# Windowed attention and a gated FFN on one core: four chunk pairs in place of three, and probabilities scaled in float32

## The chip, the cores and the metric

The kernel runs on one core of a Trainium2 chip. The metric is device time in microseconds (us), from start to end of one execution; lower is better. The engines are TensorE (PE in the profile; its weight loads are PEld), VectorE (DVE), ScalarE (ACT), GpSimd (POOL) and SyncE (SP, which here issues nearly all DMAs).

## What is computed

Attention with a window of 31 keys and block summaries (4 batches, 8 heads, 768 positions, head size 64), and behind it an FFN over the 3072 tokens (512 to 2048 to 512). Cut to what matters:

```python
k_sum = k.reshape(B, H, 24, 32, D).max(axis=3)
v_sum = v.reshape(B, H, 24, 32, D).mean(axis=3)
scores_l = scale * q @ k.T                      # kept where |i - j| < 16
scores_s = scale * q @ k_sum.T + log(32)
a = softmax(concat([scores_l, scores_s]))       # over 768 + 24 keys
x = a @ concat([v, v_sum])                      # 3072 x 512 after a transpose
h = x @ w_in                                    # 3072 x 2048
out = (h / (1 + exp(-h)) * h) @ w_out           # 3072 x 512
```

## The kernel before

**Tiling.** The tokens are 24 stages of 128 (`s`, six to a batch) and 12 chunks of 256 (`c`, two stages each). The hidden width is 8 groups of 256 (`f`). Operands that must keep more than float16 are split into a high and a low float16 part, and a product is three float16 matmuls (high by high, low by high, high by low).

**Attention** of a stage (`job_a`, `normal`, `job_c`): scores into PSUM (L697, 12 matmuls of 182 columns for four heads), a masked minimum on DVE (L708), the exponential with its sum on ACT (L711), then `normal` for two heads at a time: scale by the reciprocal of the sum into float16 (`times`, on DVE, ACT or POOL), the low part on DVE (`rest_of`, L276), a DMA transpose of both parts, and the product with V (L786). `job_v` and `v_scale` make the block means and the scale of V for a batch, `job_k` and `job_scale` those of K and Q.

**FFN.** `job_f` works one chunk and one group: the first product (L982, 24 matmuls of 256 columns), tanh on ACT (L996), a product on DVE (L997), a split on ACT and DVE or POOL, and the second product (L991, 12 of 512 columns). Chunks 0 to `WCH` - 1 go that way. From chunk `WCH` = 6 on, `pair_f` takes two chunks and one group at once: seven block products in place of eight (L1053, 42 matmuls of 256 columns where two `job_f` issue 48), with sums of blocks taken on the way (L1079, L1081, copies by L265), and the same second product (L1101). It needs sums of blocks of w_in, which `sum_w` makes once for each of the eight groups (four additions, L870, a high part on ACT and a low part on DVE), spread over the chunks from 2 to `WCH` - 1, and sums of blocks of x, made by `pair_x` for every pair.

**Order.** All steps are registered with the engines that may run them and a cost. `ORDER` is a table that fixes the engine and the place of every step; `Plan.replay` reads it and each engine's instructions are issued in that order, with warming matmuls (L391, `fill`) put where it leaves PE unused. Each engine works strictly in order, and SP issues its DMAs in order as well.

Of the kernel before, what the change touches and what calls it, by code (L numbers as in the profile page):

```python
# [21 lines left out]
P = 128  # L22
# [33 lines left out]
WCH = 6  # L56
# [198 lines left out]
def local_attn_ffn(ctx: ExitStack, tc: tile.TileContext, q0, qkT, qF, qkD, kF, v, vR, w, out):  # L255
# [118 lines left out]
    e_t = ring(NE, [P, 2, NKEY], F32, "e")  # L374
# [132 lines left out]
    def v_scale(b, prio):  # L507
        k = sbank()
# [6 lines left out]
            lambda e: nc.vector.tensor_scalar(out=sc2[:, 1:2], in0=sc2[:, 1:2], scalar1=XTOP, scalar2=None, op0=ALU.mult),  # L515
# [9 lines left out]
    def job_v(b, prio):  # L525
        prio += nudge("v", b)
        for j in range(4):
            stg, key = staging()
            vr = stg[:, :S]
            plan.op({"dma": 1020}, lambda e, vr=vr, j=j: nc.sync.dma_start(out=vr, in_=vR[b, :, j, :]), w=key, prio=prio)  # L530
            plan.op({"dve": 869}, lambda e, vr=vr, j=j: nc.vector.tensor_reduce(out=vm_t[:, j, :], in_=vr.rearrange("p (n k) -> p n k", k=BLK), axis=AX.X, op=ALU.add),
                    r=key, w=[("vm", j)], prio=prio, port=())
            plan.op({"dve": 869}, lambda e, vr=vr, j=j: nc.vector.tensor_reduce(out=am_t[:, j:j + 1], in_=vr, axis=AX.X, op=ALU.max, apply_absolute_value=True), r=key, w=[("am", j)], prio=prio, port=())
        am_sum(4, prio)
        k = sbank()
# [9 lines left out]
        v_scale(b, prio)  # L545
# [115 lines left out]
    def job_a(m, prio):  # L661
# [37 lines left out]
        if g % 2 == 0:  # L699
# [6 lines left out]
            plan.op({"pe": 600 if b else 950 if plain else 820}, scores, r=need, w=[("bank", x) for x in pair_banks], prio=prio, cols=728)  # L706
# [24 lines left out]
        for x in (m - 1, m):  # L731
            normal(x, su, sums, prio)

    def normal(m, su, sums, prio):
        n, pk = m % NE, m % NP
        et, pt = e_t[n], p_t[pk]
        er = [("e", n, 0), ("e", n, 1)]
        tt, ttk = tt_of(m)
        c0 = m % 2 * 2

        def scaled(e, i):
            by = su[:, c0 + i:c0 + i + 1]
            times(e, pt[:, i, :NKEY], et[:, i, :NKEY], by)
# [4 lines left out]
        def low(e):  # L748
            for i in range(2):
                rest_of(pt[:, i, P + 64:P + 64 + NKEY], et[:, i, :NKEY], su[:, c0 + i:c0 + i + 1], pt[:, i, :NKEY])  # L750

        plan.op({"dve": 680}, low, r=er + sums, w=[("p", pk), ("p", pk, "half")], prio=prio)
        plan.op({"dma": 672}, lambda e: nc.sync.dma_start_transpose(out=tt, in_=pt.rearrange("p a b -> p (a b)")), r=[("p", pk), ("p", pk, "half")], w=[ttk], prio=prio, cols=1230)
# [365 lines left out]
    def job_stage(s):  # L1119
# [20 lines left out]
        job_vs(s, p[0] - TUNE["vs"] if b else p[0])  # L1140
# [68 lines left out]
    "1la1lm1m900400v01100l1lz1lh01f00r00b00h1m601k01501b01p05p07007605w06q06w02y02401t02j07i06606203908j02808t03s06c08p07807p"  # L1209
    "06e0aq03d08z09102n07z08507v0200990av06l02f0re07g09i08709n0b908f0ga0d204303202u0rl0ca0bq09s0ck0dj0rr03o0d90b005g0ed04d0gf"  # L1210
    "0bg0e303h03w09x0bw0cg0dp0df0cq10a0e90ej0ru0dr0tm10n1nh0el04904g0dy10h0bm0es04n04s05l0f204x0520cs11t0b50gt0by10q0080f7057"
    "05c0a00d01nm0h00v50i40gk0tt0s00ha09b0a70tz0fc0hu0fh0hg0u20ia0i00sx0ic0s40u70h60hi0s70lu0c60fk0ik0hq1200ac0ai0im0se1261nu"
    "0fr0jn0jt0gp0it0jx0ev0ue0iz0k30j30lz0k50j91nx0km0vc0sj0kr0sp0kw0jb0l10kc0uf0l40fw0ao0ji0lb0vh0md0ta0kf0g20st0g80t40um0ux"
    "0mu0ne0nk0n01cw1410no0nu0nw12i0mk0vu0mq0n21480o40na12p0m41290v10vl0td1d11d912v0o61uk1dv14q10v0ph0w10w70pn0m91dd1dj0on0od"
    "0p70oj0pd0ot0wa0wg12y1e01dl0q60pp1up0wk0ov0pw0ut0wn0wu1120lg1ux14d0p30y20x10x51dq1330pz0qb1521e80xd0x91eu1ez0lm0qg1ec0y9"
    "1ei0yf14h0xk0ql18h0yi1f70qo0xq0qv0yo1fb1fh1ek0xt14x0tj0ys1n40r00zl1u80ls1vj1ep0yv1fo0z21v01tn0r61fj1mu0ra12f0zd1381561h2"
    "1h70zs0zh15b0vr1hf1131mn18o16916m1hj1ft1hp1fy18u1v41tq16g15i11a13b18x13i1vy1w41hw1j015j0z91g611l1ga0zy1n71ty1gg10116p363"
    "16y1751791md3681j50xz1gn10717e1ml1i11jd16v14n17j1mx15q17o1i61ie1tg1va1931gi1ii1io17r3bf3bk1hr3bn11h1vg13p13t1wd17y19736d"
    "19c1iv1jh1jn11p1831lu1uh19f19m19r19w1a11a61891wa1ab1ag18d1jz1k41o01o71ne13x1b11ju1or1kc1c51wj1x21h01cf1oh1bv1iq1yz1z41b5"
    "1ox1wp1kg1km1vp1jp1p11xc1kt20336k15x1611vv1lr1c91bz1zc1ws44e1x91zg1xs1651zm1p71zs1od1on1xj1l51qn1re1r41qu1pb4s22081wz1rk"  # L1220
# [122 lines left out]
```

## Time and profile before

| | us |
|---|---|
| median of 3 runs (605.93 to 606.89) | 606.72 |
| the profiled execution, whole | 605.51 |
| its span, first to last instruction | 603.8 |
| PE busy | 594.7 |
| PEld busy | 400.1 |
| DVE busy | 462.7 |
| ACT busy | 403.3 |
| POOL busy | 157.0 |

The share of an engine's busy time is taken over the span. Matmuls overlap, so the mean duration of one matmul is longer than the distance from one to the next; the time that a run of them takes is read from where the next piece begins.

### The profile page before, as it was taken

The numbers are of one execution on the slowest core, as the hardware profiler recorded it, in microseconds if no ns is written. First come the engines' busy times: TensorE is split into PE (matmuls) and PEld (weight loads), VectorE is DVE, ScalarE is ACT, GpSimd is POOL, SyncE is SP. The second block draws the span as 40 slices with busy tenths as digits, with TensorE's granted clock in tenths as the row PEclk, the third lists the DMA queues.
The fourth block names the chain that finished last, engine by engine and source line by source line (L and its number), as shares of the span: only waits on it lengthen the run. The fifth ranks groups of instructions, "written<-read, shape, count | busy, mean of one in ns | idle before, by whom it ended". The sixth has DMA issues, their size and how long they took to land.

```text
span 603.8 us, 13503 instructions
## 1 busy us (share of the span) xinstructions
PE 594.7 (98%) x5052; PEld 400.1 (66%) x5052; DVE 462.7 (77%) x1237; ACT 403.3 (67%) x929; POOL 157.0 (26%) x206
## 2 busy tenths in 40 slices
PE   8999999999999999999999899999999999999997
PEld 5786666676676776666676566765666765777653
DVE  7998989999878848987989689989877586464330
ACT  4999999767777577676787568677656475343321
POOL 3336412321422022313321404120333234300100
PEclk9999999999999999999999999999999999999999
DMA  8898724564596651765596355826445424000001
GB/s 324 307 403 334 311 62 145 105 216 105 134 198 125 192 187 53 211 166 96 165 216 129 121 176 127 213 79 138 151 107 160 59 81 80 36 36 1 1 1 70
DMA packets 85558, 87.88 MB, mean 146 GB/s; under 512 B 66780, under 2 KB 68828, under 8 KB 83444
## 3 DMA queue, kind: packets, MB, share of 16 engines
q1 hardware_dynamic: 85348, 86.89, 51.1%
q8 instruction: 39, 0.64, 0.4%
q14 instruction: 27, 0.22, 0.1%
q10 hardware_dynamic: 144, 0.13, 0.1%
HBM read 62.82 MB, written 6.29 MB: 114 GB/s over the span
## 4 chain that ended last, share of the span: by engine, by line
PE 93%; DMA 3%; DVE 1%; ACT 1%; issue 0%; SPq 0%
PE bank L991 22%; PE bank L1101 21%; PE bank L982 19%; PE bank L1053 18%; PE bank L786 4%; PE bank L697 3%; DMA wt<-in_w_dram 1%; PE bank L689 1%; PE bank L770 1%; DMA wt<-in_kF_dram 1%; DMA raw<-in_vR_dram 1%; PE bank L720 1%; PE bank L391 1%; DMA out_dram<-raw 1%; PE bank L611 0%; PE bank L722 0%
## 5 line engine op out<-in xcount | busy, mean ns | idle before, releaser
L991 PE MATMUL bank<-wt,g 128*128 128x512 f16 (+1 forms) x544 | 141.9, 406 | 0.8 <-ACT g L269 0.8
L982 PE MATMUL bank<-xh,wt 128*128 128x256 f16 x768 | 136.2, 273 | 0.0
L982 PEld LDWEIGHTS <-wt 128*128 128x128 f16 x1152 | 111.5, 98 | 25.0 <-issue 3.8
L1053 PE MATMUL bank<-wt 128*128 128x256 f16 x936 | 114.4, 273 | 1.1 <-DVE t L1033 0.8
L1053 PEld LDWEIGHTS <-wt 128*128 128x128 f16 x936 | 90.8, 98 | 24.9 <-issue 1.7
L982 PE MATMUL bank<-xl,wt 128*128 128x256 f16 x384 | 104.7, 273 | 0.0
L711 ACT ACTIVATE e<-e,mx 128x182 f32<-128x182 f32 x192 | 83.6, 437 | 24.3 <-DVE mx L708 22.1
L991 PEld LDWEIGHTS <-g 128*128 128x128 f16 x480 | 45.8, 98 | 47.2 <-issue 0.2
L1032 ACT ACTIVATE t<-bank,asc 128x512 f32<-128x512 f32 x48 | 32.4, 686 | 59.1 <-PE bank L1053 48.7
L279 POOL TENSOR_TENSOR g<-t,g 128x512 f16<-128x512 f32 x34 | 39.4, 1159 | 123.5 <-ACT g L1034 47.7
L1101 PE MATMUL bank<-wt,g 128*128 128x512 f16 x288 | 69.3, 379 | 0.0
L276 DVE SCALAR_TENSOR_TENSOR p<-e,sum,p 128x182 f16<-128x182 f32 x160 | 59.7, 419 | 4.2 <-ACT p L269 2.0
L708 DVE CUSTOM_DVE_ANT_0 e<-bank,masks,qsc 128x182 f32<-128x182 f32 x144 | 52.5, 401 | 3.6 <-PE bank L697 2.9
L996 ACT ACTIVATE t<-bank,asc 128x512 f32<-128x512 f32 x48 | 32.7, 681 | 28.9 <-PE bank L982 26.8
L271 POOL TENSOR_SCALAR p<-e,sum 128x182 f16<-128x182 f32 x52 | 23.1, 449 | 106.6 <-ACT t L1032 13.5
L1033 DVE SCALAR_TENSOR_TENSOR t<-t,bank 128x512 f32<-128x512 f32 x48 | 32.4, 684 | 22.1 <-ACT t L1032 21.8
L1101 PE MATMUL bank<-wt,xl 128*128 128x512 f16 x192 | 46.2, 379 | 0.0
L1101 PEld LDWEIGHTS <-g 128*128 128x128 f16 x288 | 27.6, 98 | 26.8
L997 DVE SCALAR_TENSOR_TENSOR t<-t,bank 128x512 f32<-128x512 f32 x48 | 32.7, 682 | 12.6 <-ACT t L996 12.0
L269 ACT ACTIVATE p<-e,sum 128x182 f16<-128x182 f32 x76 | 31.3, 438 | 9.1 <-DMA tt<-p 3.3
L711 ACT ACTIVATION_READ_ACCUMULATOR e<-e,mx 128x1 f32 x192 | 36.2, 189 | 0.0
L870 POOL TENSOR_TENSOR wt<-wt 128x256 f32<-128x256 f32 x20 | 14.5, 735 | 65.3 <-DVE wt L868 12.5
(206 smaller groups left out, 955.8 us busy)
## 6 DMA issues: line engine op xcount, KB each, us to landing
wt<-in_w_dram SPq DMA_DIRECT2D x16, 1024.0 KB
raw<-in_v_dram SPq DMA_DIRECT2D x20, 768.0 KB
raw<-in_qkD_dram SPq DMA_DIRECT2D x18, 572.0 KB
out_dram<-raw SPq DMA_DIRECT2D x24, 256.0 KB
raw<-in_kF_dram SPq DMA_DIRECT2D x12, 384.0 KB
raw<-in_qF_dram SPq DMA_DIRECT2D x9, 512.0 KB
raw<-in_vR_dram SPq DMA_DIRECT2D x12, 384.0 KB
raw<-vms SPq DMA_DIRECT2D x40, 48.0 KB
```

The lines of the kernel that those rows point to most:

```text
L276: nc.vector.scalar_tensor_tensor(out=out, in0=in_, scalar=by, in1=less, op0=ALU.mult, op1=ALU.subtract)
L279: eng[e].tensor_tensor(out=out, in0=in0, in1=in1, op=ALU.subtract)
L708: plan.op({"dve": 258 if b == 0 else 323}, lambda e, i=i: nc.vector.tensor_tensor_reduce(out=et[:, i, :NKEY], in0=sc[:, i, :NKEY], in1=mas ...
L711: plan.op({"act": 431}, lambda e, i=i, h=h: nc.scalar.activation(out=et[:, i, :NKEY], in_=et[:, i, :NKEY], func=AF.Exp, scale=-1.0, bias=m ...
L982: nc.tensor.matmul(out=h[:, d * CH:(d + 1) * CH], lhsT=wt[f, 0][:, part, d, ct * P:(ct + 1) * P], rhs=x[:, ct, :], start=(ct == 0 and q == ...
L991: nc.tensor.matmul(out=bank[to][:, :z0 - a0], lhsT=a[:, d * CH + u * P:d * CH + u * P + P], rhs=b[:, d, a0:z0], start=(opens and d == 0 an ...
L996: plan.op({"act": 640}, lambda e: nc.scalar.activation(out=t, in_=h, func=AF.Tanh, scale=asc_t[c // 3 % 2][:, f:f + 1]), r=[("bank", k), ( ...
L997: plan.op({"dve": 605}, lambda e: nc.vector.scalar_tensor_tensor(out=t, in0=t, scalar=1.0, in1=h, op0=ALU.add, op1=ALU.mult), r=[("bank", ...
L1032: plan.op({"act": 640}, lambda e: nc.scalar.activation(out=t, in_=h, func=AF.Tanh, scale=asc_t[c // 3 % 2][:, f:f + 1]), r=[("bank", k), ( ...
L1033: plan.op({"dve": 605}, lambda e: nc.vector.scalar_tensor_tensor(out=t, in0=t, scalar=1.0, in1=h, op0=ALU.add, op1=ALU.mult), r=[("bank", ...
L1053: nc.tensor.matmul(out=to, lhsT=w2[part][:, ct * P:(ct + 1) * P], rhs=xs[j][:, x, ct, :], start=(opens and ct == 0 and q == 0), stop=(ct = ...
L1101: nc.tensor.matmul(out=bank[to], lhsT=a[:, d * CH + v * P:d * CH + v * P + P], rhs=wt[f, 1][:, b][:, d, :], start=(opens and d == 0 and q ...
```

## The change

`WCH` goes from 6 to 4. Chunks 4 and 5 are worked by `pair_f` and `pair_x` instead of `job_f` and `job_x`, so there are four pairs (4 and 5, 6 and 7, 8 and 9, 10 and 11), and `sum_w` has its eight groups done during chunks 2 and 3, one in two `job_f` instead of one in four.

`normal` now takes four heads: four multiplications of the exponentials by their scale, in place and in float32 (DVE, ACT or POOL), one cast of all four heads to float16 (ACT or POOL) and one subtraction for the low parts (DVE or POOL). The maxima of |V| may be taken on ACT. The scale steps of Q, K (`scale_qk`) and of V (`finish_v`) for the later batches are registered behind the scores of another stage and use PSUM bank 7, and the loads of V for the first two stages of such a batch (`job_vs`) stand behind them. A factor in the scale of V goes from 2^-4 to 2^-10 for the batches from 1 on. `ORDER` is a new table.

```diff
-WCH = 6
+XSUM = 2.0 ** -10
+WCH = 4
-    e_t = ring(NE, [P, 2, NKEY], F32, "e")
+    e_all = const.tile([P, 2 * NE, NKEY], F32, name="e")
+    e_t = [e_all[:, 2 * i:2 * i + 2, :] for i in range(NE)]
...
+        if 6 * b - 2 < 2 * WCH + 4:
+            scale_qk(b, prio, 7 if b > 1 else None)
+
+    def scale_qk(b, prio, k=None):
...
-        k = sbank()
+        k = sbank() if k is None else k
...
-            plan.op({"dve": 869}, lambda e, vr=vr, j=j: nc.vector.tensor_reduce(out=am_t[:, j:j + 1], in_=vr, axis=AX.X, op=ALU.max, apply_absolute_value=True), r=key, w=[("am", j)], prio=prio, port=())
+            def bound(e, vr=vr, j=j):
+                if e == "act":
+                    nc.scalar.activation(out=vr, in_=vr, func=AF.Abs, accum_out=am_t[:, j:j + 1])
+                else:
+                    nc.vector.tensor_reduce(out=am_t[:, j:j + 1], in_=vr, axis=AX.X, op=ALU.max, apply_absolute_value=True)
+
+            plan.op({"dve": 869, "act": 830}, bound, w=key + [("am", j)], prio=prio, port=())
+        if 6 * b < 2 * WCH + 4:
+            finish_v(b, prio, 7 if b > 1 else None)
+
+    def finish_v(b, prio, k=None):
...
-        for x in (m - 1, m):
-            normal(x, su, sums, prio)
+        normal(m - 1, su, sums, prio)
...
-        for i in range(2):
-            plan.op({"dve": 240, "act": 350, "pool": 427}, lambda e, i=i: scaled(e, i), r=sums + er[i:i + 1], w=[("p", pk) + (() if i else ("half",))], prio=prio)
...
-        plan.op({"dve": 680}, low, r=er + sums, w=[("p", pk), ("p", pk, "half")], prio=prio)
+        for i in range(4):
+            plan.op({"dve": 180, "act": 340, "pool": 427}, lambda e, i=i: times(e, e4[:, i], e4[:, i], su[:, i:i + 1]), r=sums, w=es[i:i + 1], prio=prio)
+        plan.op({"act": 740, "pool": 1640}, lambda e: copy(e, hi, e4), r=es, w=[k + ("half",) for k in ps], prio=prio)
+        plan.op({"dve": 830, "pool": 1640}, lambda e: less(e, lo, e4, hi), r=es + [k + ("half",) for k in ps], w=ps, prio=prio)
...
-        job_vs(s, p[0] - TUNE["vs"] if b else p[0])
+        if not (s // 2 % 3 == 0 and s >= 2 * WCH + 4):
+            job_vs(s, p[0] - TUNE["vs"] if b else p[0])
...
+            if m == 4 * s + 3 and t == 5 and b + 1 < B and s >= 2 * WCH + 4:
+                scale_qk(b + 1, when(4 * s))
+            if m == 4 * s + 3 and t == 1 and s >= 2 * WCH + 4:
+                finish_v(b, when(4 * s))
+                for x in (s - 1, s):
+                    job_vs(x, when(4 * s))
...
 ORDER = (
...
-    "1la1lm1m900400v01100l1lz1lh01f00r00b00h1m601k01501b01p05p07007605w06q06w02y02401t02j07i06606203908j02808t03s06c08p07807p"
+    "00b00h1la01k00l01f00r01501p02400701b00405p05w00v06602y06202j06q1lu01t1lm0110re02803d07002006c06e1lh07i07603s03906m0aq0av"
```

What the table does is seen in the engines' instructions. The line numbers of the changed kernel differ: L1061 is L1053 of before, L1073 is L1065, L713 is L697, L724 is L708, L1005 is L997, L274 is L273, L280 is L279.

PE of before at the start of the pair stage (chunks 6 and 7): the end of the first two products into bank 189, a matmul that opens bank 190, and the third product into it.

```order
L1053 MATMUL bank_189<-wt,xr_169 128x256
L1053 LDWEIGHTS xr_170
L1053 MATMUL bank_189<-wt,xr_170 128x256
L1065 LDWEIGHTS ident
L1065 MATMUL bank_190<-ident 128x256
L1053 LDWEIGHTS xr_169
L1053 MATMUL bank_190<-wt,xr_169 128x256
```

PE of the changed kernel at the start of its pair stage (chunks 4 and 5), the same two products into bank 186, and what follows them.

```order
L1061 MATMUL bank_186<-wt,xr_166 128x256
L1061 LDWEIGHTS xr_167
L1061 MATMUL bank_186<-wt,xr_167 128x256
L713 LDWEIGHTS qk_137
L713 MATMUL bank_192<-qk_137 128x182
L713 LDWEIGHTS qk_137
L713 MATMUL bank_193<-qk_137 128x182
```

The 12 score matmuls of a stage now stand between the first two products and the third (into bank 187), and 12 more before the first two products of the next group; the opening matmul (L1073) stands ahead of the first two products.

DVE of before in chunk 3, while stages 8 and 9 have their probabilities made: low parts of two heads at a time (L276), beside the FFN (L997) and the masked minimum (L708).

```order
L276 SCALAR_TENSOR_TENSOR p<-e_161,sum_153,p 128x182 x2
L997 SCALAR_TENSOR_TENSOR t_184<-t_184,bank_189 128x512
L276 SCALAR_TENSOR_TENSOR p<-e_160,sum_153,p 128x182 x2
L708 ISA e_160,mx_156<-bank_191,masks,qsc_143 128x182
```

DVE of the changed kernel at that stage.

```order
L745 TENSOR_SCALAR sum_155<-sum_155 128x4
L746 RECIPROCAL sum_155<-sum_155 128x4
L274 TENSOR_SCALAR e<-e,sum_155 128x182
L280 TENSOR_TENSOR p<-e,p 128x4x182
L724 ISA e,mx_159<-bank_192,masks,qsc_143 128x182
```

Four instructions of L276 for four heads have become one of L280; of the four multiplications (L274) DVE keeps one here, and the cast ahead of L280 is on ACT.

## Rows read from the trace of the kernel before

**Rows 1.** The page, part 1 and a line of part 2: engines, granted clock.

```profile
PE 594.7 (98%) x5052; PEld 400.1 (66%) x5052; DVE 462.7 (77%) x1237; ACT 403.3 (67%) x929; POOL 157.0 (26%) x206
...
PEclk9999999999999999999999999999999999999999
```

**Rows 2.** The chain that ended last, by engine.

```profile
PE 93%; DMA 3%; DVE 1%; ACT 1%; issue 0%; SPq 0%
```

**Rows 3.** Pieces of that chain at 193 us: start, length, what.

```profile
193.17 1.31 PE bank L982 x12
194.48 1.29 PE bank L991 x6
195.78 1.31 PE bank L982 x12
```

**Rows 4.** PE's groups by form: count, busy us, mean ns of one, idle before.

```profile
L982 PE MATMUL bank<-xh,wt 128*128 128x256 f16 x768 | 136.2, 273 | 0.0
L1053 PE MATMUL bank<-wt 128*128 128x256 f16 x936 | 114.4, 273 | 1.1 <-DVE t L1033 0.8 <-DVE bank L265 0.3
...
L391 PE MATMUL bank<-ident 128*128 128x256 bf16 x60 | 9.7, 324 | 1.4 <-POOL ident masks.py:199 1.4
```

**Rows 5.** Timeline of PE around one block of scores: start, length, what.

```profile
236.37 1.46 PE L991 MATMUL bank<-wt,g 128*128 128x512 f16 x6
237.76 0.65 PE L697 MATMUL bank<-qk 64*128 64x182 f16 x12
238.34 0.28 PE L982 MATMUL bank<-xh,wt 128*128 128x256 f16 x1
```

**Rows 6.** Timeline of PE at the start of the pair stage, idle time in brackets.

```profile
334.40 5.35 PE L991 MATMUL bank<-wt,g 128*128 128x512 f16 x24
...
341.92 0.83 PE L1053 MATMUL bank<-wt,xr 128*128 128x256 f16 x6 [0.75 <-DVE bank L265]
...
343.27 0.83 PE L1053 MATMUL bank<-wt,xr 128*128 128x256 f16 x6 [0.53 <-DVE bank L1079]
...
346.91 1.47 PE L1053 MATMUL bank<-wt 128*128 128x256 f16 x12 [0.84 <-DVE t L1033]
```

**Rows 7.** PE's waits: us in total, times, longest.

```profile
PE bank L991 <- ACT g L269: 0.8, 1, 0.8
```

**Rows 8.** Windows: us, busy (instructions) of PE, PEld, DVE, ACT, POOL, clock, DMA.

```profile
110.00:230.00 120.00, 119.95 (x1099) 81.78 (x1097) 99.42 (x260) 84.73 (x198) 27.87 (x41) 1.00 0.62 159
230.00:340.00 110.00, 110.00 (x1012) 73.91 (x1011) 90.88 (x251) 78.47 (x191) 30.44 (x39) 1.00 0.62 149
340.00:440.00 100.00, 97.87 (x879) 65.53 (x879) 87.20 (x250) 72.28 (x179) 24.42 (x27) 1.00 0.54 143
```

**Rows 9.** DVE's groups by form, columns as in rows 4.

```profile
L276 DVE SCALAR_TENSOR_TENSOR p<-e,sum,p 128x182 f16<-128x182 f32 x160 | 59.7, 419 | 4.2 <-ACT p L269 2.0 <-POOL p L271 2.0
...
L279 DVE TENSOR_TENSOR g<-t,g 128x512 f16<-128x512 f32 x30 | 20.7, 692 | 7.1 <-ACT g L1034 3.9 <-ACT g L1001 2.9
...
L533 DVE TENSOR_REDUCE am<-raw 128x1 f32<-128x768 f32 x12 | 11.3, 946 | 0.1
...
L273 DVE TENSOR_SCALAR p<-e,sum 128x182 f16<-128x182 f32 x32 | 9.4, 309 | 0.9 <-DMA tt<-p 0.6
L729 DVE TENSOR_SCALAR sum<-sum 128x4 f32<-128x4 f32 x40 | 7.4, 184 | 3.4 <-ACT e L711 3.4
...
L868 DVE TENSOR_TENSOR wt<-wt 128x1024 f32<-128x1024 f16 x2 | 2.4, 1218 | 0.0
```

**Rows 10.** ACT's groups by form.

```profile
L269 ACT ACTIVATE p<-e,sum 128x182 f16<-128x182 f32 x76 | 31.3, 438 | 9.1 <-DMA tt<-p 3.3 <-DVE sum L730 2.5 <-ACT e L711 2.1
...
L269 ACT ACTIVATE wt<-wt,ur 128x1024 f16<-128x1024 f32 x13 | 14.9, 1142 | 1.1 <-POOL wt L870 0.9 <-DVE ur L924 0.2
...
L460 ACT ACTIVATE raw<-raw 128x768 f32<-128x768 f32 x12 | 10.0, 835 | 2.1 <-DVE km L457 1.9
```

**Rows 11.** POOL's groups by form.

```profile
L279 POOL TENSOR_TENSOR g<-t,g 128x512 f16<-128x512 f32 x34 | 39.4, 1159 | 123.5 <-ACT g L1034 47.7 <-ACT g L1001 21.5 <-DVE p L276 16.3
```

More of the change, by code (lines that the diff above doesn't have):

```diff
@@ L505, in out_scale, with v_scale @@
         plan.op({"pool": 250, "dve": 130}, lambda e: times(e, osc_t[b % 2], kap_t[:, 1:2], vsc_t[b % 2][:, 1:2]), r=["kap", ("vsc", b % 2)], w=[("osc", b % 2)], prio=prio)
-    def v_scale(b, prio):
-        k = sbank()
+    def v_scale(b, prio, k=None):
+        k = sbank() if k is None else k
         plan.op({"pe": 220}, lambda e, k=k: nc.tensor.matmul(out=bank[k][:, :P], lhsT=am_t[:, 7:8].to_broadcast([P, P]), rhs=ident, start=True, stop=True), r=["am4"], w=[("bank", k)], prio=prio, cols=512)
@@ L514, in v_scale @@
             lambda e: nc.vector.tensor_scalar(out=sc2[:, 1:2].bitcast(U32), in0=sc2[:, 0:1].bitcast(U32), scalar1=0x7F800000, scalar2=None, op0=ALU.bitwise_and),
-            lambda e: nc.vector.tensor_scalar(out=sc2[:, 1:2], in0=sc2[:, 1:2], scalar1=XTOP, scalar2=None, op0=ALU.mult),
+            lambda e: nc.vector.tensor_scalar(out=sc2[:, 1:2], in0=sc2[:, 1:2], scalar1=XSUM if b else XTOP, scalar2=None, op0=ALU.mult),
             lambda e: nc.vector.reciprocal(out=vs[:, 0:1], in_=sc2[:, 1:2]),
@@ L532, in job_v @@
                     r=key, w=[("vm", j)], prio=prio, port=())
-            plan.op({"dve": 869}, lambda e, vr=vr, j=j: nc.vector.tensor_reduce(out=am_t[:, j:j + 1], in_=vr, axis=AX.X, op=ALU.max, apply_absolute_value=True), r=key, w=[("am", j)], prio=prio, port=())
+            def bound(e, vr=vr, j=j):
[7 more added lines that the diff above has]
+    def finish_v(b, prio, k=None):
         am_sum(4, prio)
-        k = sbank()
+        k = sbank() if k is None else k
         def tr(e, k=k):
@@ L705, in job_a @@
                 need += [("qkm", s % 2, hp) for hp, _ in heads(g)]
-            plan.op({"pe": 600 if b else 950 if plain else 820}, scores, r=need, w=[("bank", x) for x in pair_banks], prio=prio, cols=728)
+            plan.op({"pe": 660 if b else 950 if plain else 820}, scores, r=need, w=[("bank", x) for x in pair_banks], prio=prio, cols=728)
         for i, (hp, h) in enumerate(heads(g)):
@@ L730, in job_a @@
         plan.op({"dve": 75}, lambda e: nc.vector.reciprocal(out=su, in_=su), w=sums, prio=prio)
-        for x in (m - 1, m):
-            normal(x, su, sums, prio)
+        normal(m - 1, su, sums, prio)
     def normal(m, su, sums, prio):
         n, pk = m % NE, m % NP
[L736 to L743, printed above, removed]
-        for i in range(2):
-            plan.op({"dve": 240, "act": 350, "pool": 427}, lambda e, i=i: scaled(e, i), r=sums + er[i:i + 1], w=[("p", pk) + (() if i else ("half",))], prio=prio)
-        def low(e):
-            for i in range(2):
-                rest_of(pt[:, i, P + 64:P + 64 + NKEY], et[:, i, :NKEY], su[:, c0 + i:c0 + i + 1], pt[:, i, :NKEY])
-        plan.op({"dve": 680}, low, r=er + sums, w=[("p", pk), ("p", pk, "half")], prio=prio)
-        plan.op({"dma": 672}, lambda e: nc.sync.dma_start_transpose(out=tt, in_=pt.rearrange("p a b -> p (a b)")), r=[("p", pk), ("p", pk, "half")], w=[ttk], prio=prio, cols=1230)
+        es, ps = [("e", n + x, i) for x in range(2) for i in range(2)], [("p", pk + x) for x in range(2)]
+        e4 = e_all[:, 2 * n:2 * n + 4, :]
+        p4 = p_all[:, pk * 2 * UW:(pk + 2) * 2 * UW].rearrange("p (a b) -> p a b", a=4)
+        hi, lo = p4[:, :, :NKEY], p4[:, :, P + 64:P + 64 + NKEY]
+        for i in range(4):
+            plan.op({"dve": 180, "act": 340, "pool": 427}, lambda e, i=i: times(e, e4[:, i], e4[:, i], su[:, i:i + 1]), r=sums, w=es[i:i + 1], prio=prio)
+        plan.op({"act": 740, "pool": 1640}, lambda e: copy(e, hi, e4), r=es, w=[k + ("half",) for k in ps], prio=prio)
+        plan.op({"dve": 830, "pool": 1640}, lambda e: less(e, lo, e4, hi), r=es + [k + ("half",) for k in ps], w=ps, prio=prio)
+        for x in range(2):
+            tt, ttk = tt_of(m + x)
+            plan.op({"dma": 672}, lambda e, tt=tt, x=x: nc.sync.dma_start_transpose(out=tt, in_=p_t[pk + x].rearrange("p a b -> p (a b)")), r=[ps[x], ps[x] + ("half",)], w=[ttk], prio=prio, cols=1230)
     def job_c(m, prio):
@@ L1213 @@
[L1213 to L1220, printed above, removed]
@@ L1276 @@
+    "9xd9vi9vm9zj9zl9fm9t79xi9vs9vw9ya9zs9zva029qp9qu9vz9tm9tha0a9w49ye9yk9yoa12a16a1c9w99z1a1ga2da059we9xq9xu9y09y4a0i9yw9z6"
+    "a2k9yra0ma0sa2oa2sa30a33a0wa1ja1ya1ra1ua25a29")
 NUDGE = {}
```

122 lines of the change are left out of this document (65 added, 57 removed).

## The prediction, made before the result was known

> **What bounds the kernel now.** The page's busy shares come first: TensorE 98%, VectorE 77%, ScalarE 67%, GpSimd 26%, the granted clock full in all 40 slices, which is the level of 2.4 GHz [rows 1]. A busy TensorE need not be one at its peak, so the second view is the chain that ended last: 93% of the span is TensorE [rows 2]. The third is that chain in order of time: twelve matmuls of 256 columns begin at 193.17 us, the next piece at 194.48, the one behind it at 195.78 [rows 3]. That is 1.31 us for twelve, 0.109 each (256 columns at 2.4 GHz are 0.107), and 0.216 for one of 512. The pieces stand without a gap, so outside the start and a few named waits the end moves by what is taken out of TensorE's row of instructions, and by nothing else. TensorE sat idle 0.75, 0.53 and 0.84 us where the pair stage begins [rows 6] and 0.8 us once for ScalarE early on [rows 7]; from 110 to 340 us it was busy 229.95 of 230 [rows 8].
>
> A page of the Trainium skill speaks against this reading: Perfetto Trace Analysis (section Identifying the Most-Contended Engine) wants TensorE judged by the share of its weight loads and not by busy matmuls. That share is 66% [rows 1], below VectorE's 77%, so by the page VectorE would be the engine to look at. The trace's abutting pieces [rows 3] speak for TensorE. It is the last rival below.
>
> **Matmuls removed.** Two chunks and one group cost 48 matmuls of 256 columns in the first product as two single chunks and 42 as a pair. Over eight groups that is 48 fewer, and the two orders agree: the sum of all 256-column matmuls falls by 48 besides the warming ones. 48 x 0.109 = 5.24 us less, all on the path, at 230 to 340 us, where TensorE had no idle time [rows 8]. The second product keeps its count. The new order also has 4 warming matmuls fewer, 56 for 60; they stand where TensorE waits, so I count 0, with 4 x 9.7/60 = 0.65 us as the bound [rows 4].
>
> **Blocks of scores and V products.** At a change from 128-row to 64-row matmuls the stream loses something: six of 512 columns begin at 236.37, would be through at 237.67, and the scores begin at 237.76 [rows 5], 0.09 us. Coming back I put the same (an estimate), 0.19 for a block. Counted in the two orders, 44 such blocks stand apart before and 47 now: 3 x 0.19 = +0.57.
>
> **The start of the pair stage.** Before, nothing stands between the dependent products of the first group and TensorE waits 2.12 us [rows 6]. Now twelve scores stand in the first gap and twelve more ahead of the second group's first products. One block takes 0.67 (0.09 and the 0.58 to 238.34 [rows 5]); two cover 1.34 of the 0.75 and 0.84. These scores stood on the path elsewhere, so I take -1.34; bounds -2.12 (no wait left) and 0 (the scores wait for stage 12's operands, and the gap stays). The first products need stage 10 and 11's V product and its sums; in the order 9.1 us of TensorE work stand between, where before 5.35 sufficed without a wait [rows 6].
>
> **Probabilities.** For 40 times four heads VectorE loses 160 low parts (59.7 us), 32 multiplications (9.4) and 12 maxima of |V| (11.3) [rows 9]. It gets 54 multiplications to float32 and 29 low parts of 728 columns. No row shows the first: 0.309 for the same size into float16 is the upper bound and 0.184 for four columns the lower [rows 9]; I take 0.25, the middle. A low part lies between 0.692 for 512 and 1.218 for 1024 columns [rows 9]: 0.91 by the line through them. So -80.4 + 13.5 + 26.4 = -40 us; the fourth pair's additions, 16 of 256 and 7 of 512 columns at no more than 0.69 each, give back up to 16. ScalarE loses 76 multiplications (31.3 us) and gets 57 at the same 0.41 and 36 casts of 728 columns, under the 0.835 for 768 [rows 10], I take 0.80, and 12 maxima at 0.835: +31 us, and up to 10 for the fourth pair. GpSimd gets 11 low parts at 1.159 x 728/512 = 1.65 [rows 11] and 4 casts at no more than that: up to +25. None of this is on the path while TensorE does not wait.
>
> Here VectorE: DVE Perf Modes (Mode 2x_2P) of the Trainium skill bears on the multiplication: float32 to float32 in SBUF goes at two columns a cycle, 182/2/0.96 = 95 ns of streaming, an estimate, beside the fixed part. By that the 54 would cost near the lower bound, 9.9 us instead of 13.5. No run shows it yet.
>
> The chain for four heads gets longer, since one cast and one low part wait for all four and both transposes stand behind them on SP: a cast (0.80) and up to 1.65 of GpSimd more. Its cover is TensorE's work between the last scores of a stage and the V product that reads them. Laid out with the distances of rows 3 and 5, the least is 12 us in the old order and 15 in the new. The loads and scale steps of V moved behind the scores have 11 us of TensorE work for batch 3 (from the matmul that spreads the maxima to the V product) and 18 for batch 2. Both hide the chain; without cover, one V product would wait 2 to 3 us.
>
> **Weight sums in half the time.** Eight groups are summed in chunks 2 and 3 instead of 2 to 5, and score work is drawn forward. Counted in the orders between the 12th and 32nd first product (about 110 to 230 us), ScalarE gets some 25 us more: 14 casts (11.2), 11 exponentials (4.8, at the 0.438 of a multiplication of that size), 6 weight passes (6.9 at 1.142), 3 maxima (2.5) [rows 10]. VectorE gets some 7 more. They had 35.3 and 20.6 us idle there [rows 8], so both fit, ScalarE closely. I take +0.5 for TensorE's waits, bounds 0 and +3.
>
> **The start.** The first 60 us are in another order; the one wait there that a good order could take is 0.8 [rows 7]. I take 0, with 1 us to either side.
>
> **Sum.** -5.24 + 0.57 - 1.34 + 0.5 = -5.51. The profiled execution took 605.51 (span 603.8, 1.71 around it), so 600.0; the median of the runs is 1.21 above that execution, which gives **601.2**. With all bounds low, -5.24 - 0.65 - 2.12 - 1 + 0.57 = -8.4, 598.3; with all high, -5.24 + 0.57 + 3 + 1 = -0.7, 606.0.
>
> **Rivals.** *ScalarE fills up in chunks 2 and 3* (the slower one). Idle time of an engine in strict order is not all usable, since part of it is waiting for TensorE's banks. If half of ScalarE's 35.3 us can be used, 17.7 of the 25.4 fit and TensorE waits 7.7: 601.2 - 0.5 + 7.7 = 608.4. It turns slower than before once more than 7.2 us don't fit. Against it: VectorE had 99.4 of 120 us busy there and 90.9 of 110 behind it [rows 8] while TensorE lost 0.05. For it: ScalarE would come to 110 of 120. Chance 0.12.
>
> *The pairs' own chain gives the gain back.* Each group of a pair has two handovers on which TensorE waits for VectorE, hidden by other matmuls in nearly all of the 24 groups of before (L1053 shows 1.1 us idle in its main form [rows 4]). If each of the eight new groups, which run beside attention, shows one of 0.53 [rows 6] and the two fills don't come: 601.2 + 4.2 + 1.3 = 606.7, no change. Against it: the later pairs also run beside attention, and TensorE was busy 97.87 of 100 us there, the first group's 2.12 being all of the loss [rows 8]. Chance 0.07.
>
> *TensorE is not the limit* (the page's reading): the 5.2 us go from an engine with time to spare, and the end stays at 606.7. Rows 3 speak against it. Chance 0.04.
>
> **Chances and range.** The forecast has 0.77. What a measurement of this kernel can tell from no change is about 0.2%, 1.2 us: below 605.5 is faster, above 607.9 slower. Faster 0.77, same 0.07 + 0.04 = 0.11, slower 0.12. The range takes in the forecast's bounds and the two rivals at no change, 598.6 to 606.7; the slower rival and the last of the low end stay out.
>
> **What would show it.** Right: 48 fewer matmuls of 256 columns at 0.109; the pair stage begins near 235 us with waits under 1 us; low parts of 728 columns near 0.9 us; TensorE without gaps from 110 us to the end of the first pair. Wrong: TensorE idle behind ScalarE or VectorE between 110 and 235 us, or a repeated wait of half a microsecond in every group of chunks 4 and 5, or a start longer by more than 1 us.

## The result, and the profile after

The changed kernel takes 599.29 us (median of 7 runs, 598.63 to 603.7), the kernel before 606.55 (7 runs, 605.9 to 606.89): a ratio of 0.9896, 95% interval 0.987 to 0.9921. Forecast were 601.2 and a range of 598.6 to 606.7. By the medians that is 7.26 less, and the profiled execution went from 605.51 to 598.76, 6.75 less, where the sum said 5.51.

The page of the changed kernel, parts 1 and 4 (beside [rows 1, 2]):

```profile
PE 589.0 (99%) x5000; PEld 394.5 (66%) x5000; DVE 444.3 (74%) x1155; ACT 433.0 (73%) x982; POOL 177.8 (30%) x218
...
PE 61%; DMA 4%; DVE 4%; ACT 2%; SPq 1%; issue 1%; DVEq 0%
```

52 matmuls are gone, 48 of the products and 4 that warm. VectorE has 18 us less to do, ScalarE 30 and GpSimd 21 more. TensorE is as full as it was, but in this execution the chain that ended last passes through other engines and transfers more often. In a second profiled execution of the same kernel (600.13 us) TensorE has 86% of it, so that share moves from run to run. Where the chain leaves TensorE is part of what the experiments showed.

The same stretches as in [rows 8]:

```profile
110.00:230.00 120.00, 119.31 (x1100) 80.07 (x1099) 104.81 (x272) 105.60 (x249) 35.82 (x44) 1.00 0.67 165
230.00:340.00 110.00, 108.57 (x1006) 73.02 (x1005) 86.43 (x231) 82.22 (x194) 35.67 (x37) 1.00 0.50 132
340.00:440.00 100.00, 99.63 (x864) 66.46 (x862) 74.92 (x207) 75.14 (x181) 30.68 (x38) 1.00 0.54 147
```

ScalarE got 20.9 us more between 110 and 230 us and VectorE 5.4, and TensorE lost 0.69 of 120. The pairs begin at 244.86 us, where TensorE's timeline reads (start, length, what, idle time in brackets):

```profile
246.27 0.65 PE L713 MATMUL bank<-qk 64*128 64x182 f16 x12
247.19 0.83 PE L1061 MATMUL bank<-wt,xr 128*128 128x256 f16 x6 [0.28 <-DVE bank L266]
248.55 0.83 PE L1061 MATMUL bank<-wt,xr 128*128 128x256 f16 x6 [0.53 <-DVE bank L1087]
...
251.28 0.65 PE L713 MATMUL bank<-qk 64*128 64x182 f16 x12
252.19 1.47 PE L1061 MATMUL bank<-wt 128*128 128x256 f16 x12 [0.26 <-DVE t L1041]
```

The scores stand in two of the three gaps of [rows 6], and these shrink from 0.75 and 0.84 to 0.28 and 0.26. The middle one keeps its 0.53 to the digit. Together 2.12 became 1.07. Smaller waits came up beside them: 0.12 and 0.23 us right behind (254.20 and 255.47 us) and 0.37 at 356.42, where the kernel before had 0.28 at 440.66. From 110 us to the end TensorE is idle 2.47 us in all, and before it was 2.40.

One wait is new. TensorE and VectorE at 203 us:

```profile
202.93 0.59 PE L999 MATMUL bank<-wt,g 128*128 128x512 f16 x2
204.21 1.04 PE L999 MATMUL bank<-wt,g 128*128 128x512 f16 x4 [0.68 <-DVE g L280]
```

```profile
202.04 1.28 DVE L277 SCALAR_TENSOR_TENSOR wt<-wt,ur 128x1024 f16<-128x1024 f32 x1
203.24 0.31 DVE L274 TENSOR_SCALAR e<-e,sum 128x182 f32<-128x182 f32 x1
203.47 0.69 DVE L280 TENSOR_TENSOR g<-t,g 128x512 f16<-128x512 f32 x1
```

The low part of a hidden value stands behind 1.28 us of weight work, now drawn into this stretch, and a multiplication.

### The profile page after: what moved, and what is told of

It reads as the page before. It is cut to its first block, busy times and chain, and to the rows that moved or that the text cites. A ratio compares the mean times of both kernels' runs of the same rounds, so it can differ in the third digit from the quotient of the medians.

```text
span 597.0 us, 13372 instructions
## 1 busy us (share of the span) xinstructions
PE 589.0 (99%) x5000; PEld 394.5 (66%) x5000; DVE 444.3 (74%) x1155; ACT 433.0 (73%) x982; POOL 177.8 (30%) x218
## 4 chain that ended last, share of the span: by engine, by line
PE 61%; DMA 4%; DVE 4%; ACT 2%; SPq 1%; issue 1%; DVEq 0%
PE bank L1109 27%; PE bank L1061 23%; PE bank L999 3%; PE bank L794 3%; PE bank L990 3%; PE bank L713 2%; DMA raw<-in_qkD_dram 2%; SPq L761 1%; DMA raw<-in_kF_dram 1%; DVE p L280 1%; DMA out_dram<-raw 1%; DVE e L724 1%; DMA raw<-in_vR_dram 1%; ACT e L727 1%; DVE km L459 0%
## 5 line engine op out<-in xcount | busy, mean ns | idle before, releaser
L1061 PE MATMUL bank<-wt 128*128 128x256 f16 x1248 | 151.7, 273 | 0.9 <-DVE bank L1089 0.4
L1061 PEld LDWEIGHTS <-wt 128*128 128x128 f16 x1248 | 121.2, 98 | 32.4 <-issue 1.3
L999 PE MATMUL bank<-wt,g 128*128 128x512 f16 (+1 forms) x352 | 96.7, 418 | 0.7 <-DVE g L280 0.7
L1109 PE MATMUL bank<-wt,g 128*128 128x512 f16 x396 | 94.7, 379 | 0.1
L990 PE MATMUL bank<-xh,wt 128*128 128x256 f16 x512 | 90.8, 273 | 0.0
L990 PE MATMUL bank<-xl,wt 128*128 128x256 f16 x256 | 69.8, 273 | 0.0
L724 DVE CUSTOM_DVE_ANT_0 e<-bank,masks,qsc 128x182 f32<-128x182 f32 x144 | 53.0, 402 | 8.2 <-PE bank L713 7.0
L280 POOL TENSOR_TENSOR g<-t,g 128x512 f16<-128x512 f32 x25 | 28.9, 1157 | 78.2 <-ACT g L1042 14.8
L272 POOL TENSOR_SCALAR e<-e,sum 128x182 f32<-128x182 f32 x49 | 25.3, 522 | 87.8 <-DVE sum L746 28.8
L1109 PEld LDWEIGHTS <-xl 128*128 128x128 f16 x240 | 22.9, 98 | 21.9 <-issue 0.2
L262 ACT CAST p<-e 128x728 f16<-128x728 f32 x36 | 28.6, 793 | 5.4 <-POOL e L272 2.7
L1109 PE MATMUL bank<-wt,xh 128*128 128x512 f16 x132 | 31.8, 379 | 0.0
L280 DVE TENSOR_TENSOR p<-e,p 128x728 f16<-128x728 f32 x29 | 28.0, 965 | 4.1 <-ACT p L262 2.9
L280 POOL TENSOR_TENSOR xl<-t,xl 128x512 f16<-128x512 f32 x13 | 15.1, 1158 | 43.0 <-ACT xl L1042 21.7
```

The costliest lines, as they stand in the source:

```text
L262: nc.scalar.copy(out=out, in_=in_)
L272: nc.gpsimd.tensor_scalar(out=out, in0=in_, scalar1=by, scalar2=0.0, op0=ALU.mult, op1=ALU.add)
L280: eng[e].tensor_tensor(out=out, in0=in0, in1=in1, op=ALU.subtract)
L724: plan.op({"dve": 258 if b == 0 else 323}, lambda e, i=i: nc.vector.tensor_tensor_reduce(out=et[:, i, :NKEY], in0=sc[:, i, :NKEY], in1=mas ...
L990: nc.tensor.matmul(out=h[:, d * CH:(d + 1) * CH], lhsT=wt[f, 0][:, part, d, ct * P:(ct + 1) * P], rhs=x[:, ct, :], start=(ct == 0 and q == ...
L999: nc.tensor.matmul(out=bank[to][:, :z0 - a0], lhsT=a[:, d * CH + u * P:d * CH + u * P + P], rhs=b[:, d, a0:z0], start=(opens and d == 0 an ...
```

## Experiments

Each run went beside runs of the kernel before on the same chip (their medians are 605.72, 605.77 and 606.05 us), and a ratio is taken to these. Differences from the 599.29 of the changed kernel are across chips; its own ratio is 0.9896 (0.987 to 0.9921).

**Are the 48 matmuls the gain?** From both sides: the changed kernel with the 48 put back, and the kernel before with as many left out (the second one leaves a part of the product out).

```diff
# e1, in the pairs' first product
+            if c == 4:
+                product(1, left[0], True)
             product(1, left[0], True)
...
# e2, in the kernel before: 3 of 24 matmuls less in each first product of chunks 4 and 5
+                cts = NCT - 1 if c in (4, 5) and d == 0 else NCT
-                for ct in range(NCT):
+                for ct in range(cts):
...
```

> The changed kernel with six more matmuls of 256 columns in each of the eight groups of chunks 4 and 5: the first product of a group is issued twice, the first time for nothing. All other instructions and their order stay. If the gain is the 48 matmuls taken out of TensorE's row, the time goes from 599.3 back by 48 x 0.109 = 5.2 us, to 604.5. If TensorE has time to spare there and the gain is the relief of VectorE, or the new order elsewhere, it stays within 1 us of 599.3.

> The kernel before with three of the 24 matmuls of each first product of chunks 4 and 5 left out (the last quarter of the sum over the 512 inputs in one half), 48 in all; its order stays. TensorE's row as the limit: 606.6 - 5.2 = 601.3, and what the new order and the new form of the probabilities are worth is then the 2 us from there to 599.3. If the helpers set the time in the old order: 605 to 606.5.

Measured: 603.96 us with them put back (10 runs, 602.26 to 605.54; ratio to before 0.9973, 0.9959 to 0.9988), and 600.98 with them left out (4 runs, 600.56 to 600.99; 0.9918, 0.9904 to 0.9933). That is +4.7 and -4.8 us, 0.098 and 0.100 for one matmul, where the sum had 0.109; their intervals, 0.9 us either way and more, take in its 5.24. The row of TensorE's instructions sets the end, in the old order and in the new. By the ratios, what the change does besides is worth 1.3 us (0.9918 to 0.9896), which the intervals do not tell from nothing.

**What does the old form of the probabilities cost in the new order?** The changed kernel, its order kept, with the multiplications writing float16 themselves and four low parts of 182 columns on VectorE in place of one of 728 on VectorE (29 times) or GpSimd (11 times).

```diff
# what the planned steps call; the steps themselves stay
-  times(e, e4[:, i], e4[:, i], su[:, i:i + 1])
+  times(e, hi[:, i], e4[:, i], su[:, i:i + 1])
-  copy(e, hi, e4)
+  None
-  less(e, lo, e4, hi)
+  [rest_of(lo[:, i], e4[:, i], su[:, i:i + 1], hi[:, i]) for i in range(4)]
```

> The changed kernel with the old form of the probabilities: the four multiplications write float16 at once, no cast, and four low parts of 182 columns on VectorE for every four heads (160 in place of 40 of 728 columns on VectorE or GpSimd). VectorE gets some 30 us more of its 444, ScalarE 29 less, GpSimd 20 less. If the new form only shifts work that is hidden, the time stays or rises by up to 3 us, with waits of TensorE for VectorE between 110 and 340 us. If the new form is what makes room for the fourth pair, it rises by 5 us or more.

Measured: 614.04 us (4 runs, 613.42 to 614.65; ratio 1.0135, 1.012 to 1.0151), 14.7 above the changed kernel. So the new form, which I had put beside the path, is needed in this order. VectorE has 472.3 us of work, 28 more, but the run also sets a form into an order made for another, so it does not tell the relief from the fit; the next experiments bear on that. Its stretches and TensorE's longest waits (us, times, longest):

```profile
110.00:230.00 120.00, 116.83 (x1081) 78.33 (x1079) 110.53 (x306) 94.71 (x233) 36.80 (x44) 1.00 0.64 164
230.00:340.00 110.00, 104.16 (x957) 69.22 (x955) 88.27 (x245) 73.85 (x175) 25.98 (x29) 1.00 0.47 119
```

```profile
PE bank L1061 <- DVE bank L1087: 4.2, 4, 1.8
PE bank L713 <- DVE mx L724: 4.0, 4, 1.6
PE bank L1061 <- DVE t L1041: 1.8, 2, 1.6
PE bank L1061 <- DVE bank L266: 1.6, 3, 1.1
```

VectorE has 21.7 us idle of 110 between 230 and 340 us, and TensorE loses 5.8 there all the same. It waits for single results, the longest times 1.1 to 1.8 us, and not for an engine that is full.

**And the new form in the old order?** The kernel before, pairs and weights as they were, with the new form. For each four heads the cast was put on ScalarE behind the last multiplication, the low part and the transposes behind it; the rest of the order stayed, but for 7 score steps that had to move.

```diff
-        for x in (m - 1, m):
-            normal(x, su, sums, prio)
+        normal(m - 1, su, sums, prio)     # with the normal() of the changed kernel
```

> The kernel before, its pairs, weights and order untouched, but with the probabilities in their new form (multiplied in float32, four heads' cast in one ScalarE instruction, four heads' low part in one VectorE instruction). By the prediction none of that is on the path: 604.5 to 607.5 us, no change against the kernel before, with VectorE some 40 us and more less busy. If the form is worth time by itself: 603 us or less. If the casts on ScalarE come too late for the transposes: above 608 us, with TensorE waiting for them.

Measured: 632.33 us (4 runs, 631.03 to 633.88; ratio 1.0441, 1.0416 to 1.0465). That is the third case, by 26 us. What VectorE and TensorE wait for (longest first):

```profile
DVE p L279 <- ACT p L261: 29.7, 25, 3.4
```

```profile
PE bank L779 <- DMA tt<-p: 7.1, 4, 3.6
PE bank L540 <- DVE vm L532: 3.2, 1, 3.2
PE bank L1046 <- DVE t L1026: 2.7, 2, 1.9
```

VectorE, in strict order, stands 29.7 us before low parts whose cast is not there yet, and what is queued behind them comes late to TensorE; the transposes are late too. In all TensorE is idle 23.2 us, where the kernel before has 5.0. What is left of the 26 stands beside a granted clock of 0.99 over the run, where the kernel before has 1.00. Being less busy (444.4 us for 462.7, where 40 and more was expected) is worth nothing then.

**Is that the form's price, or that of an order made for the other form?** Three kernels without the table of the order, so that the planner's own sweeps place everything anew: the kernel before, the same with the new form, and the changed kernel.

```diff
-ORDER = (
-...
-)
+ORDER = ()
```

> The kernel before without its table of the order, so that the planner's own sweeps set it. No forecast of its level; it is the base for the two below. By the waits that a hand-made order takes out, 615 to 680 us.

> The kernel before with the new form of the probabilities, ordered by the planner's own sweeps. If the form is as unsuited by itself as it looked in the old order (26 us slower), over 15 us slower than the one above. If that loss was the old order's, which has no place for the casts: within 8 us of it, either way.

> The changed kernel (fourth pair, new form) ordered by the planner's own sweeps. By the matmuls, 5.2 us less than the one with the new form alone; with the planner's order worth a few us of chance either way, 0 to 12 us less. A fourth pair that needs the table would not be faster than that one.

Measured: 660.32 us (659.22 to 660.87), 668.23 (667.62 to 675.85) and 663.34 (662.12 to 664.92), 4 runs each. Placed anew, the form costs 7.9 us, and the fourth pair, with the steps moved for it, takes 4.9 away. That is near the 5.2 of its matmuls, but it does not measure them: TensorE is idle 44.2, 45.6 and 42.7 us in these three, and their granted clocks are 0.979, 0.964 and 0.957. So by these orders the form alone does not make the kernel faster, and some 18 of the 26 us would be the old order's (an estimate); the sweeps' own luck of a few us is in both numbers. The table is worth 55 us before and 64 after (660.32 - 605.72 on this chip, 663.34 - 599.29). The whole change under the planner is slower than before by 3 us.

**Two moves meant to take the waits away.** The changed kernel with the low part of 203.47 us ahead of the weights on VectorE, and six matmuls of the last single group, with their output copy on ScalarE, put into the pair's middle gap.

```diff
# VectorE
+L280 TENSOR_TENSOR g_183<-t_181,g_183 128x512
 L277 SCALAR_TENSOR_TENSOR wt<-wt,ur 128x1024
 L274 TENSOR_SCALAR e<-e,sum_153 128x182
-L280 TENSOR_TENSOR g_183<-t_181,g_183 128x512
# ScalarE: the copy behind four exponentials and the pair's first tanh
 L270 ACTIVATE raw_134<-bank_191,osc_99 128x512
+...
+L1040 ACTIVATE t_181<-bank_186,asc_93 128x512
 L270 ACTIVATE raw_134<-bank_190,osc_99 128x512
```

> The changed kernel with two moves in the order. In chunk 3 the low part of g (L280) goes ahead of a weight low part (L277, 1.28 us) and of a multiplication on VectorE, where TensorE waited 0.68 us by the profile. At the start of the pair stage the last six second products of chunk 3 go from ahead of the pair into the gap behind its third product, where TensorE waited 0.53 us. If these waits are on the path and nothing else is late behind them, 1.2 us less, 598.1; if the helpers are behind anyway, the waits come back a few us later and the time stays at 599.3.

Measured: 606.68 us (10 runs, 604.45 to 607.66; ratio 1.0011, 0.9997 to 1.0025), 7 slower than the changed kernel. Neither theory holds. The waits of 0.68 and 0.53 are gone, but the first gap at the pairs' start grew from 0.28 to 0.79. And the trace has one wait of 5.0 us for the low part at L280, which led to the next kernel.

**One ScalarE copy, 0.68 us, alone.** TensorE's row and VectorE's are those of the changed kernel.

```diff
# ScalarE
 L270 ACTIVATE raw_134<-bank_191,osc_99 128x512
+L865 CAST wt<-wt 128x512
+...
+L1040 ACTIVATE t_181<-bank_186,asc_93 128x512
 L270 ACTIVATE raw_134<-bank_190,osc_99 128x512
```

> The changed kernel with a single ScalarE copy moved: the output copy of chunk 3 (0.68 us at L1033, whose output row is written next) stands behind the first tanh of the pair of chunks 4 and 5. TensorE does not wait for that copy. Theory that the write, the V transfer into the same buffer, the V reduction and the low part behind it on VectorE are one chain: 604 to 607.5 us, with a wait of TensorE of 4 to 5 us for the low part at about 255 us, as in the kernel with the two moves. Rival that the matmuls moved there, or the VectorE exchange at 204 us, made that kernel slow: 598.6 to 600.3 us.

Measured: 606.08 us (10 runs, 604.37 to 608.12; ratio 1.0007, 0.9992 to 1.0022). The copy alone costs what the two moves cost, as the theory of one chain had it. Its trace on SP, VectorE and TensorE:

```profile
245.38 7.96 SPq L1035 DMA_DIRECT2D out_dram<-raw  x2
255.08 0.82 SPq L536 DMA_DIRECT2D raw<-in_vR_dram  x2
```

```profile
258.58 0.95 DVE L537 TENSOR_REDUCE vm<-raw 128x24 f32<-128x768 f32 x1 [5.47 <-DMA raw<-in_vR_dram]
259.45 0.68 DVE L280 TENSOR_TENSOR g<-t,g 128x512 f16<-128x512 f32 x1
```

```profile
260.19 1.68 PE L1109 MATMUL bank<-wt,g 128*128 128x512 f16 x4 [5.13 <-DVE g L280]
```

Read down: the copy comes late, so the second half of chunk 3's output leaves late; V is loaded into the same buffer and waits until it is out; VectorE waits 5.47 us for V; the low part of the pair's hidden value is queued behind that reduction; TensorE waits 5.13. The granted clock falls after it:

```profile
255.00:260.00 5.00, 0.06 (x1) 0.00 (x0) 1.42 (x2) 0.44 (x1) 0.00 (x0) 1.00 0.52 159
260.00:265.00 5.00, 4.81 (x19) 2.46 (x20) 4.51 (x15) 3.45 (x12) 2.64 (x3) 0.66 0.35 117
265.00:270.00 5.00, 5.00 (x41) 3.73 (x39) 3.44 (x9) 4.30 (x10) 0.76 (x1) 1.00 0.06 6
```

TensorE did 0.06 us of work in the first stretch, and in the next its mean clock is 0.66, between the level of 1.2 and that of 2.4 GHz; then it is full again. A third of 5 us is 1.7, which with the wait of 5.13 makes 6.8, what the copy cost (an estimate). The four matmuls at 260.19 take 1.68 us, where the changed kernel's four of that width at 204.21 take 1.04.

In the changed kernel the same two transfers abut, and VectorE still waits 0.46 us for the second. They are two of the places where its chain that ended last leaves TensorE (start, length, what):

```profile
245.67 3.54 DMA out_dram<-raw
249.27 3.31 DMA raw<-in_vR_dram
```

**Do those transfers make the runs differ?** The changed kernel once more, the same with that reduction of V moved behind the low part, and the one with VectorE's exchange at 202 us alone.

```diff
# e7, VectorE
+L280 TENSOR_TENSOR g_183<-t_181,g_183 128x512
+L1041 SCALAR_TENSOR_TENSOR t_182<-t_182,bank_187 128x512
 L537 TENSOR_REDUCE vm<-raw_134 128x24
-L280 TENSOR_TENSOR g_183<-t_181,g_183 128x512
-L1041 SCALAR_TENSOR_TENSOR t_182<-t_182,bank_187 128x512
# e12, VectorE: the first of the two moves above, alone
```

> The changed kernel itself, beside the three runs below on the same chip: 599.3 us and a spread of about 5 us, as it had (598.6 to 603.7 in 7 runs). If the spread comes from one place where a late transfer is waited for, some runs lie near 598.7 and single ones 1 to 5 us above.

> The changed kernel with one reduction of V (the one at 252.59 us, which waits 0.46 us for its transfer in front of the low part of the hidden value) moved behind that low part and the next hidden value on VectorE, its maxima on ScalarE behind the next cast. Theory that VectorE's queue behind this transfer is the sensitive place: median up to 0.5 us lower than the changed kernel's, and its runs closer together, within about 1.5 us. Rival that the spread comes from elsewhere: same spread, 598.6 to 603.7, same median.

> The changed kernel with one move on VectorE: at 202 us the low part of the hidden value (0.69 us) ahead of the second layer's low part of the weights (1.28 us) and of one multiplication (0.31 us). Theory that the wait of 0.68 us at 204.21 us is what the weight sums in half the time cost: it goes, and 0.7 to 0.85 us with it: 598.0 us where the changed kernel has 598.8 to 599.3. Rival that the next thing on the way is as late: no difference.

Measured: 598.76 us (4 runs, 598.11 to 600.13), 599.03 (5 runs, 598.46 to 599.91) and 600.59 (6 runs, 598.32 to 601.56). Moving the reduction changes nothing that can be told: its runs lie within 1.5 us, as the theory had it, but the changed kernel's beside them lie within 2.0. The exchange does its part: its six matmuls begin at 203.85 and run through.

```profile
203.85 1.46 PE L999 MATMUL bank<-wt,g 128*128 128x512 f16 x6
205.24 0.65 PE L713 MATMUL bank<-qk 64*128 64x182 f16 x12
```

But the kernel is not 0.8 us faster: its median is 1.3 us higher, on another chip, and the ratios, 0.9913 (0.9897 to 0.9928) and the changed kernel's 0.9896, do not tell the two apart. Its profiled run shows two other waits. One comes 7 us on, for a low part on GpSimd; the kernel with the two moves, which has the same exchange, shows 0.42 there, and neither profile of the changed kernel has a wait for GpSimd at that place. So the next thing on the way is late too, as the rival had it.

```profile
210.73 1.04 PE L999 MATMUL bank<-wt,g 128*128 128x512 f16 x4 [0.40 <-POOL g L280]
```

For the other, V came later than in the changed kernel's run, and VectorE and TensorE waited:

```profile
254.39 0.95 DVE L537 TENSOR_REDUCE vm<-raw 128x24 f32<-128x768 f32 x1 [1.51 <-DMA raw<-in_vR_dram]
```

```profile
256.00 1.04 PE L1109 MATMUL bank<-wt,g 128*128 128x512 f16 x4 [1.16 <-DVE g L280]
```

The changed kernel's second profile (600.13 us) shows 0.6 for the same wait and one of 0.7 in front of the scale steps of q and k (L483 behind VectorE's L475, at 230.13 us), after a cast of ScalarE that waited 1.5 us for a transpose; its first (598.76) shows 0.1 and none. The first is a fortunate one early on too: of the six other profiles with nearly this order, five wait 0.30 to 0.88 us near 8 us for a load (wt<-in_v_dram), and five 0.34 to 0.56 us near 47 us for ScalarE. So single transfers that land a little later are part of why two profiles of one kernel differ by 1.4 us, and by that a candidate for why its runs spread over 5 us where those of before spread over 1 to 2.6. Whether they are all of it, and whether the exchange made V later or met it late by chance, these runs do not settle. The exchange with the reduction moved as well was not tried. The moved scale steps and loads of V were not tried alone either. None of these versions beats the changed kernel.

## Why the prediction was right, step by step

- **What bounds the kernel**: right, and shown by both kernels with 48 matmuls more and less. By the rival that took TensorE for an engine with time to spare, following Perfetto Trace Analysis of the Trainium skill (section Identifying the Most-Contended Engine), they would not have moved; weight loads are 66% of the span in both kernels, below VectorE's 77% and 74%. In this kernel that share does not name the bound. But I gave half of the section: it names MFU, the matmul work over the window at peak speed, beside the share of weight loads. Counted as columns of a full array of 128 by 128 at 2.4 GHz, the matmuls of the kernel before, the warming ones left out, fill 519 of 603.8 us, 86% (an estimate), above VectorE's 77%. So the page as a whole does not speak against the reading, and the rival was weaker than I had it.
- **Matmuls removed, -5.24**: 4.7 and 4.8 us by the two experiments. This term carries the prediction, mechanism and size.
- **Blocks of scores, +0.57**: +0.56, counted from the starts of successive matmuls: all distances into, within and out of the blocks of scores and V products, less the waits and less what the FFN's matmuls take at their usual spacing. Blocks are 44 and 47, as counted in the orders.
- **Start of the pair stage, -1.34**: -1.05. The step that was off: I counted 0.67 of cover for each block of scores, with the 0.09 that the stream loses at the change of rows. They covered 0.47 and 0.58, the second just its own length from [rows 5]. And what the three gaps gave went again in the small waits named above. My "near 235 us" for the start was 10 us early; no term hung on it.
- **Weight sums in half the time, +0.5**: 0.68 in one wait, at 204.21 us (0.36 in the kernel's second profile). By the prediction's own list an idle TensorE there was a sign of being wrong; it was one wait of the size that the sum had. The price of ScalarE (+25 us in chunks 2 and 3) was +20.9, VectorE's +7 was +5.4.
- **Warming matmuls and the start, 0**: TensorE's first matmul of the FFN comes at 39.1 us, before at 39.6.
- **What the sum missed**: 1.24 us of gain by the profiled executions, 1.75 by the medians. From the starts of successive matmuls, TensorE's row is 6.34 shorter: 5.24 by count, 0.56 longer by blocks, 0.72 less in waits, and 0.95 that the traces do not place; behind the last matmul it is 0.4 less again. The 0.72 is not the -1.34 + 0.5 of the sum: from 110 us on the waits came out even (2.40 and 2.47), and what went is mainly the wait of 0.77 us at 47.91 [rows 7], which the sum had left in and which stands in most other profiles of the new order, at 0.34 to 0.56. So beside the matmuls the forecast came near by terms that made up for each other, and that part is luck.
- **Durations**: the cast of 728 columns was put at 0.80 and takes 0.793; the low part at 0.91 and takes 0.965; ScalarE's +31, with up to 10 more for the fourth pair, is +30; GpSimd's up to 25 is 21. VectorE's are these:

```profile
L280 DVE TENSOR_TENSOR p<-e,p 128x728 f16<-128x728 f32 x29 | 28.0, 965 | 4.1 <-ACT p L262 2.9 <-POOL p L264 0.7
...
L274 DVE TENSOR_SCALAR e<-e,sum 128x182 f32<-128x182 f32 x54 | 16.5, 328 | 0.3
...
L262 ACT CAST p<-e 128x728 f16<-128x728 f32 x36 | 28.6, 793 | 5.4 <-POOL e L272 2.7 <-DMA tt<-p 0.8 <-DVE t L1005 0.5
```

The float32 multiplication takes 0.328 in the mean, above my upper bound of 0.309 [rows 9], but 50 of the 54 lie between 0.285 and 0.318 and four between 0.38 and 0.81; the median is 0.313. The new form relieves VectorE by 35.9 us, where I had 40. Of these 17.5 went back, to the fourth pair's additions and to steps that the new table put on VectorE, so that it has 18 less in all; I had up to 16 going back. With the old form in the new order 54 such multiplications write float16 and take 0.326, so the type of the output makes no difference here:

```profile
L274 DVE TENSOR_SCALAR p<-e,sum 128x182 f16<-128x182 f32 x54 | 16.4, 326 | 3.4 <-DMA tt<-p 3.1
```

By VectorE: DVE Perf Modes of the Trainium skill (Mode 2x_2P) the multiplication would stream 95 ns. I let that end near 0.18, but 0.184 is what four columns take [rows 9]; with 95 ns on top it is near 0.28, and with one column a cycle, 190 ns, it would be near 0.37 (both estimates). The 0.313 lies between, so the trace does not tell whether the mode was taken.
- **"None of this is on the path"**: the step that the runs correct. In the changed kernel TensorE waits little, and the sum came out, but as a reason it fails: with the old form in the new order the kernel takes 14.7 us more, and 9.0 of TensorE's lost time lie between 110 and 340 us, where [rows 8] had shown 20.6 and 19.1 us of VectorE idle. I read cover from idle shares, and the room is the distance between one result and the instruction that reads it.
- **ScalarE fills up**: did not happen (105.6 of 120 us busy). Its mechanism, work queued ahead of a result that TensorE needs, did happen on VectorE, at a tenth of the price (0.68 for 7.7).
- **The pairs' own chain**: did not give the gain back; the new pairs beside attention show no repeated wait of 0.5, and 340 to 440 us went from 97.87 to 99.63 busy, since the pair's start moved out of it.

## What to carry to other kernels

On a kernel whose bounding engine runs without gaps, count its instructions at the spacing seen in the trace: two measurements gave that term to within a tenth. The cover of the other steps can't be read from another engine's idle share, but only from the distance between one result and its reader. The two orders here, made by hand, each held such distances for one form of the work alone, so try a form and an order together, or both with the order made anew. And before a small instruction is moved, follow what it lets go (a buffer, a write, the next load) through every queue: 0.68 us of copying, on no critical path, cost 7 us here.

## What the runs showed of the hardware

- VectorE multiplies 182 float32 columns by a value per partition in 0.313 us into float32 (median of 54), no faster than into float16, 0.310 (median of the 32 of [rows 9]).
- After TensorE had done 0.06 us of work in 5 us, its granted clock was 0.66 of full over the next 5 us, and 1.00 again in the 5 us behind it: the kernel with that wait of 5.13 us took 6.8 us longer.
- One output write of 128x512 float32 took 3.54 us in one run, and the load into the same buffer began when it was through (245.67, 3.54 long; 249.27). In the run with the late copy it took 2.0 (issued at 252.99, the wait for it over at 255.04).
